# Loading the last of 32 output-weight blocks in two parts, ahead of the blocks before it

## The chip, the cores and the metric

The kernel runs on one core of one Trainium2 chip. The metric is the device time of one execution in microseconds (us); of several executions the median is taken.

## What is computed

One decoding step of an attention layer over a window of the key and value cache, times a gate from a small gated network. All data are float32. Batch B is 2, one query position, width D = 512, 32 query heads of 128, 8 key heads; the window is the last W = 4096 positions of 32768.

```python
def _A_ref(x, k_cache, v_cache, wq, wo):            # Hq 32, Dh 128
    q = (x @ wq).reshape(B, 1, Hq, Dh).transpose(0, 2, 1, 3)
    k = jnp.repeat(k_cache[:, :, Sk - W:, :], rep, axis=1)
    v = jnp.repeat(v_cache[:, :, Sk - W:, :], rep, axis=1)
    p = softmax(einsum("bhqd,bhkd->bhqk", q, k) * Dh ** -0.5)
    o = einsum("bhqk,bhkd->bhqd", p, v)
    return o.transpose(0, 2, 1, 3).reshape(B, 1, Hq * Dh) @ wo      # wo: 4096 x 512
s = _A_ref(layernorm(x), ...)
g = silu(_B_ref(layernorm(x), w_in, w_sp, b_sp, w_out))             # gated MLP, 512 -> 1792 -> 512
return x + s * g
```

The change concerns the last product, the attention output of 4096 numbers per batch entry by wo.

## The kernel before, in words

Everything is read once from memory and streamed through on-chip buffers. Large loads are issued by SyncE (SP) alone, in this order: wq in two halves, w_in, w_out, then for eight "units" (a unit is one batch entry and two key heads) a 4 MB load of keys and one of values, the values of a unit one step behind the keys, and at last wo. All of them go into a ring of four 32 KB-per-partition buffers (`slot`, L81), so that a load can be issued only when the buffer four loads earlier is free. wo's first buffer is the one that unit 5's values used, its second the one of unit 7's keys, its third the one of unit 6's values.

For each unit VectorE transposes the keys in 32x32 squares (`turn`), TensorE makes partial scores (`shares`, `add_shares`), VectorE and ScalarE make the softmax (`share_max`, `probs`), and TensorE weighs the values (`values`), after which ScalarE scales the result (`scale_out`) and TensorE adds it up by heads (`collect`). `gather` (L396) puts the output of one batch entry into `oT`: partition p, column n of its 32 columns holds row 32p + n of the 4096 rows of wo that it meets. It does so with four small TensorE products and one VectorE copy (L404 to L407). A "block" n of wo is therefore the 128 rows 32p + n, one for each partition, 256 KB; block n's product is `oT[:, n, :]` (128 x 32) by a tile of 128 x 512.

The loads of wo are written at L422 to L434: pieces of 8 and 8 blocks in the first buffer, 8 in the second, and 4, 2, 1 and 1 in the third. After the sixteenth block a 4 KB load of x stands in the queue (`x4`, L434).

The tail of the kernel (L480 to L501) uses two forms of the product:

- For blocks 0 to 27 (`EARLY = 28`) a block's product of 512 columns is added in one of four groups of 32 output rows of the tile `part`, group n % 4. ScalarE then copies `part` to `parts`, and `spread_quarters` (L276) adds the four groups with eight short products into `so`, 128 columns to a group.
- For blocks 28 to 31 four products of 128 columns each go straight to `so`. Blocks 28 and 29 stand before `spread_quarters`, blocks 30 and 31 behind it (`LATE = 30`).

VectorE multiplies `so` by the gate and adds x (`res`, L499 and L500), and SP stores 4 KB.

The order on each engine is the order of the program: `pe`, `dve`, `act` and `sp` are wrappers (`InOrder`, L27) that pass each call on and keep it in program order. For that reason the profile gives nearly all instructions the same line, L37, and groups are told apart by the names of their tiles. Each float32 product shows in the trace as two MATMUL records with a LDWEIGHTS record each: 28 blocks are 56 records of `part`.

Of the kernel before, what the change touches and what calls it, by code (L numbers as in the profile page):

```python
# [9 lines left out]
F32 = mybir.dt.float32  # L10
AF = mybir.ActivationFunctionType
# [3 lines left out]
P = 128  # L15
HQ, DH = 32, 128
G = 4
# [4 lines left out]
def ap(t, offset, dims):  # L22

    return bass.AP(tensor=t.tensor, offset=t.offset + offset, ap=[list(t.ap[0])] + [list(d) for d in dims])
# [18 lines left out]
def kernel(  # L43
# [13 lines left out]
    nc = tc.nc  # L57
    pe, dve, act, sp = (InOrder(tc, e) for e in (nc.tensor, nc.vector, nc.scalar, nc.sync))
    B, _, D = x.shape
# [17 lines left out]
    cst = ctx.enter_context(tc.tile_pool(name="cst", bufs=1))  # L77
# [3 lines left out]
    def slot(name):  # L81
        return ring.tile([P, SLOT], F32, tag="slot", name=name)

    def const(name, *shape):
        return cst.tile([P, *shape], F32, tag=name, name=name)

    def bank(name, tag):
        return ps.tile([P, 512], F32, tag=tag, name=name, bufs=BANKS[tag])
# [6 lines left out]
    for a in range(2):  # L95
        t = slot(f"wq{a}")
# [13 lines left out]
    def by_group(t):  # L110

        return bass.AP(tensor=t.tensor, offset=t.offset, ap=[[DC, G], [D, B], [1, DC]])
# [11 lines left out]
    ident = const("ident", P)  # L124
# [13 lines left out]
    place = const("place", 3 + P)  # L138
    nc.gpsimd.memset(place, 0.0)
    heads = const("heads", DH)  # L140
    oT = const("oT", 32, 32)
    nc.gpsimd.memset(oT, 0.0)

# [58 lines left out]
    for k in range(KT):  # L202
        for r in range(2):
            for g in range(G):
# [3 lines left out]
                    start=(k == 0), stop=(k == KT - 1),  # L208
# [19 lines left out]
    for k in range(KT):  # L228
        for g in range(G):
            pe.matmul(  # L230
                pz[32 * g : 32 * g + 32, :], xnT[:, k, :], ap(win[:, k, :], g * FQ, [[FH, 2], [1, FQ]]),
                start=(k == 0), stop=(k == KT - 1),
# [43 lines left out]
    def spread_quarters(dst, shares, start=True, stop=True):  # L276
        for g in range(G):
            pe.matmul(
                dst[32 * g : 32 * g + 32, :], rowm, shares[:, g * DC : (g + 1) * DC], start=start, stop=stop,
            )  # L280

    yp = bank("y", "sh")
    for j in range(FT):
        g = j % G
# [10 lines left out]
    dve.tensor_mul(gate, gate, y)  # L295


    def q_of(u, dq):
        return ap(qbd, (u.n * 4 + dq) * 32, [[1, 32]])

# [11 lines left out]
    def shares(u, m):  # L312

        u.sh = bank(f"sh{u.n}_{m}", "sh")
        for dq in range(4):
            pe.matmul(
                u.sh[32 * dq : 32 * dq + 32, :], q_of(u, dq), u.kt[m][:, :, 32 * dq : 32 * dq + 32],
                start=True, stop=True,
            )
        u.shs[m] = sb.tile([P, 512], F32, tag="shs", name=f"shs{u.n}_{m}")  # L320
        act.activation(u.shs[m], u.sh, AF.Copy)
# [99 lines left out]

    wo_v = wo.rearrange("(p j) d -> p j d", j=32)  # L422
    blocks = []
    pieces = ((8, 8), (8,), (4, 2, 1, 1))
    j = 0
    for i, piece in enumerate(pieces):
        t = slot(f"wo{i}").rearrange("p (j d) -> p j d", d=D)
        at = 0
        for n in piece:
            sp.dma_start(t[:, at : at + n, :], wo_v[:, j : j + n, :])  # L430
            blocks += [(t, at + a) for a in range(n)]
            at, j = at + n, j + n
            if j == 16:
                sp.dma_start(x4[0:P:16, :], by_group(x))  # L434

    prev = old = None
    last = units[-1]
# [39 lines left out]
    gather(last)  # L477


    EARLY, LATE = 28, 30  # L480
    part = bank("part", "sh")
    for n in range(EARLY):
        t, a = blocks[n]
        g = n % G
        pe.matmul(part[32 * g : 32 * g + 32, :], oT[:, n, :], t[:, a, :], start=(n < G), stop=(n >= EARLY - G))
    parts = sb.tile([P, D], F32, tag="shs", name="parts")
    act.activation(parts, part, AF.Copy)
    so = bank("so", "mo")[:, :DC]
    for n in range(EARLY, 32):
        if n == LATE:  # L490
            spread_quarters(so, parts, start=False, stop=False)
        t, a = blocks[n]
        for g in range(G):
            pe.matmul(
                so[32 * g : 32 * g + 32, :], oT[:, n, :], t[:, a, g * DC : (g + 1) * DC],
                start=(n == EARLY), stop=(n == 31),
            )
    res = const("res", DC)
    dve.tensor_mul(res, so, gate)  # L499
# [30 lines left out]
```

## Time and profile before

| What | Value |
|---|---|
| median of 3 runs | 217.53 us (217.28 to 217.55) |
| the profiled execution's own time | 217.5 us |
| its span, first to last instruction | 215.7 us |
| mean granted TensorE clock | 0.856 of full |
| read from memory | 89.40 MB |
| busy share of the span: TensorE, VectorE, ScalarE | 72%, 50%, 20% |

A row of the timeline has the start in us from the span's start, the duration from the first to the last end of the merged instructions, the engine (PE is TensorE, PEld its weight loads, DVE VectorE, ACT ScalarE, SPq the queue of SyncE), the operation, what it writes and reads, and in brackets how long the engine was idle before and what ended that. A row of the windows gives for each stretch of time the busy time of each engine, the granted TensorE clock, the share of time that the core's 16 DMA engines were busy, and GB/s.

### The profile page before, as it was taken

The page shows a single profiled execution, that of the slowest core. Times are in us where ns is not written, and L with a number is a line of the kernel's source. Part 1 is how long each engine was busy: PE and PEld are TensorE (multiplying, and loading weights), DVE is VectorE, ACT ScalarE, POOL GpSimd, SP SyncE. Part 2 cuts the span into 40 slices and gives each one's busy share as a digit, 9 for nine tenths or more (in the row PEclk, how much of TensorE's full clock was granted, in tenths as well). Part 3 has the DMA queues.
Part 4 walks back from the last instruction along what each step waited for, and adds up shares of the span by engine and source line. Part 5 has one row for each costly group of instructions (what it writes and reads, how often), then busy time and mean ns, then how long its engine had stood idle before and what let it go on. Part 6 is the DMA issues. An engine that isn't in the chain of part 4 may idle for free.

```text
span 215.7 us, 2229 instructions
## 1 busy us (share of the span) xinstructions
PE 155.7 (72%) x866; PEld 43.6 (20%) x866; DVE 108.5 (50%) x176; ACT 44.1 (20%) x109; POOL 2.6 (1%) x14
## 2 busy tenths in 40 slices
PE   0164856151796997899699599459959948998883
PEld 0110212110121222222122222222212212231311
DVE  3400072425976944963946851685577089240101
ACT  5000001401123115114303404120431421242001
POOL 4000000000000000000000000000000000000000
PEclk9999788755589699799889879958988995999699
DMA  7998999999999999999999999999999999999990
GB/s 292 389 486 389 425 433 454 451 416 431 444 395 474 395 459 413 450 425 431 437 400 456 413 444 428 431 437 431 431 407 453 419 444 431 431 401 416 425 377 35
DMA packets 3929, 89.54 MB, mean 415 GB/s; under 512 B 446, under 2 KB 462, under 8 KB 848
## 3 DMA queue, kind: packets, MB, share of 16 engines
q1 hardware_dynamic: 3912, 89.40, 96.8%
q8 instruction: 7, 0.11, 0.2%
q14 instruction: 2, 0.02, 0.0%
q10 hardware_dynamic: 8, 0.00, 0.0%
HBM read 89.40 MB, written 0.00 MB: 414 GB/s over the span
## 4 chain that ended last, share of the span: by engine, by line
DMA 44%; PE 31%; DVE 19%; issue 3%; ACT 1%; SPq 0%; DVEq 0%
DMA k<-in_A_k_cache_dram 22%; DMA win<-in_B_w_in_dram 14%; DVE kt L37 13%; PE s L37 9%; PE sh L37 9%; DMA wo<-in_A_wo_dram 8%; PE acc L37 6%; PE z L37 2%; PE y L37 2%; PE mo L37 1%; DVE gate L37 1%; PE col L37 1%; PE so L37 1%; DVE u L37 1%; DVE m L37 1%
## 5 line engine op out<-in xcount | busy, mean ns | idle before, releaser
L37 DVE STREAM_TRANSPOSE kt<-k 128x2048 f32<-128x2048 f32 x32 | 72.4, 2293 | 24.9 <-DMA k<-in_A_k_cache_dram 24.9
L37 PE MATMUL sh<-kt,qbd 128*32 128x512 f32 x256 | 41.5, 682 | 14.0 <-DVE kt L37 14.0
L37 PE MATMUL s<-shs,add_dq 128*128 128x512 f32 x64 | 41.0, 748 | 0.0
L37 ACT ACTIVATE shs<-sh 128x512 f32<-128x512 f32 x32 | 19.1, 597 | 100.9 <-PE sh L37 100.9
L37 PE MATMUL acc<-v,pT 128*32 128x512 f32 x256 | 32.0, 641 | 0.2 <-DVE pT L37 0.2
L37 PE MATMUL q_ps<-wq,xnT 128*32 128x512 f32 x64 | 11.0, 850 | 9.9 <-DMA wq<-in_A_wq_dram 9.9
L37 PEld LDWEIGHTS s<-shs,add_dq 128*128 128x128 f32 x64 | 11.2, 219 | 28.3 <-issue 23.9
L37 PEld LDWEIGHTS sh<-kt,qbd 128*32 128x32 f32 x256 | 6.9, 115 | 33.9 <-issue 19.6
L37 PEld LDWEIGHTS acc<-v,pT 128*32 128x32 f32 x256 | 7.7, 118 | 25.8 <-issue 23.0
L37 DVE TENSOR_REDUCE m<-s 128x2 f32<-128x512 f32 x8 | 5.4, 680 | 14.0 <-PE s L37 14.0
L37 PE MATMUL mo<-l,same_r 128*128 128x2 f32 x16 | 3.5, 287 | 10.7 <-ACT p L37 10.7
L37 DVE STREAM_TRANSPOSE qT<-q_ps 128x512 f32<-128x512 f32 x2 | 1.4, 717 | 18.1 <-PE q_ps L37 18.1
L37 ACT ACTIVATE o<-acc,wd 128x128 f32<-128x128 f32 x32 | 9.1, 373 | 3.4 <-PE acc L37 3.4
L37 ACT ACTIVATE p<-s,nb 128x256 f32<-128x256 f32 x16 | 7.6, 490 | 7.1 <-DVE nb L37 6.9
L37 PE MATMUL part<-wo,oT 128*32 128x512 f32 x56 | 8.2, 722 | 1.1 <-DMA wo<-in_A_wo_dram 0.8
L37 PE MATMUL col<-o,sel 128*32 128x512 f32 x16 | 8.3, 601 | 0.4 <-ACT o L37 0.4
L37 ACT ACTIVATE zs<-z 128x448 f32<-128x448 f32 x1 | 0.5, 544 | 30.9 <-PE z L37 30.9
L37 PE MATMUL y<-wout,hT 128*32 128x512 f32 x14 | 3.6, 1059 | 3.8 <-issue 3.8
L37 PEld LDWEIGHTS q_ps<-wq,xnT 128*32 128x32 f32 x64 | 2.6, 144 | 17.1 <-issue 12.2
L37 DVE STREAM_TRANSPOSE pT<-p 128x512 f32<-128x512 f32 x8 | 5.4, 675 | 1.2 <-ACT p L37 1.2
L37 DVE TENSOR_TENSOR res<-so,gate 128x128 f32<-128x128 f32 x1 | 0.3, 292 | 11.1 <-PE so L37 11.1
L37 ACT ACT_TABLE_LOAD x4 | 5.1, 1283 | 1.9 <-issue 1.9
(106 smaller groups left out, 66.8 us busy)
## 6 DMA issues: line engine op xcount, KB each, us to landing
k<-in_A_k_cache_dram SPq DMA_DIRECT2D x8, 4096.0 KB, 21.3
v<-in_A_v_cache_dram SPq DMA_DIRECT2D x8, 4096.0 KB, 26.7
wq<-in_A_wq_dram SPq DMA_DIRECT2D x2, 4096.0 KB, 21.3
wo<-in_A_wo_dram SPq DMA_DIRECT2D x3, 2048.0 KB
win<-in_B_w_in_dram SPq DMA_DIRECT2D x1, 3584.0 KB, 29.3
wout<-in_B_w_out_dram SPq DMA_DIRECT2D x1, 1792.0 KB, 33.1
wo<-in_A_wo_dram SPq DMA_DIRECT2D x1, 1024.0 KB
wo<-in_A_wo_dram SPq DMA_DIRECT2D x1, 512.0 KB, 17.4
```

The source lines that it names most:

```text
L37: return self.tc.keep_in_program_order(call(*args, **kwargs))
```

## The change

Block 31 no longer comes last and no longer as one load of 256 KB.

- `woe` is a tile of 128 x 512 that GpSimd clears at the start; block 31's rows of the even partitions (64 rows, 128 KB) are loaded into its even partitions.
- `woo` is a tile of 32 partitions with two rows of 512 each; the rows of the odd partitions (64 rows, 128 KB) are loaded there, two to a partition. The load's source is written as 8 x 8 rows, the outer step 64 rows and the inner 512 rows.
- Both loads are issued behind the second buffer's 8 blocks and ahead of the third buffer's pieces, which are now 4, 2 and 1 blocks.
- The first sixteen blocks are one load of 4 MB in place of two of 2 MB.
- `odd` is a matrix of zeros and ones that ScalarE copies from the identity once, behind the gate. After the last `gather`, two products with it pick the odd partitions of `oT[:, 31, :]` in the order of `woo`, and ScalarE copies each result to `oTo`.
- Block 31 moves from the short form to the long one: three products (even rows with `woe`, and two of 32 rows with `woo`) are added to `part` behind block 27, in groups 0, 1 and 2. Behind `spread_quarters` only block 30 is left.

```diff
+    woe = const("woe", D)
+    nc.gpsimd.memset(woe, 0.0)
+    woo = cst.tile([G * 8, 2, D], F32, tag="woo", name="woo")
+    oTo = const("oTo", 2, 32)
+    odd = const("odd", 2, 8, G)
     oT = const("oT", 32, 32)
     nc.gpsimd.memset(oT, 0.0)
...
+    act.activation(odd, ap(ident, 1, [[16, 2], [2, 8], [32, G]]), AF.Copy)
...
-    pieces = ((8, 8), (8,), (4, 2, 1, 1))
+    pieces = ((16,), (8,), (4, 2, 1))
...
             if j == 16:
                 sp.dma_start(x4[0:P:16, :], by_group(x))
+            if j == 24:
+                sp.dma_start(woe[0:P:2], wo_v[0:P:2, 31, :])
+                sp.dma_start(
+                    woo.rearrange("p s d -> p (s d)"),
+                    bass.AP(tensor=wo.tensor, offset=wo.offset + 63 * D, ap=[[64 * D, 8], [512 * D, 8], [1, D]]),
+                )
...
+    for a in range(2):
+        t = bank(f"oTo{a}", "acc")[: G * 8, :32]
+        pe.matmul(t, odd[:, a].rearrange("p o i -> p (o i)"), oT[:, 31, :], start=True, stop=True)
+        act.activation(oTo[: G * 8, a, :], t, AF.Copy)
     EARLY, LATE = 28, 30
+    early = [(oT[:, n, :], blocks[n][0][:, blocks[n][1], :]) for n in range(EARLY)]
+    early += [(oT[:, 31, :], woe)] + [(oTo[: G * 8, a, :], woo[:, a, :]) for a in range(2)]
     part = bank("part", "sh")
-    for n in range(EARLY):
-        t, a = blocks[n]
+    for n, (o, w) in enumerate(early):
         g = n % G
-        pe.matmul(part[32 * g : 32 * g + 32, :], oT[:, n, :], t[:, a, :], start=(n < G), stop=(n >= EARLY - G))
+        pe.matmul(part[32 * g : 32 * g + 32, :], o, w, start=(n < G), stop=(n >= len(early) - G))
     parts = sb.tile([P, D], F32, tag="shs", name="parts")
     act.activation(parts, part, AF.Copy)
     so = bank("so", "mo")[:, :DC]
-    for n in range(EARLY, 32):
+    for n in range(EARLY, 31):
...
-                start=(n == EARLY), stop=(n == 31),
+                start=(n == EARLY), stop=(n == 30),
```

## The prediction

> **What bounds the kernel now.** I read the page first, its slices of time and its chain, then the timeline of the tail, then the tail in windows of half a microsecond, and last SP's own timeline.
>
> ```profile
> span 215.7 us, 2229 instructions
> DMA  7998999999999999999999999999999999999990
> HBM read 89.40 MB, written 0.00 MB: 414 GB/s over the span
> ```
>
> The DMA engines are busy in all slices but the last. The kernel is a stream of 89.40 MB at 414 GB/s with a tail behind it, so what an edit in the last loads is worth is decided behind the point at which that stream thins out. The tail in the timeline (the first columns are the start and the duration):
>
> ```profile
> 200.07 1.07 PE L37 MATMUL oT<-heads,place 32*128 32x32 f32 x8 [0.78 <-DVE heads L37]
> 201.18 0.21 DVE L37 COPY oT<-oT 128x32 f32<-128x32 f32 x1 [1.17 <-PE oT L37]
> 201.49 5.24 PE L37 MATMUL part<-wo,oT 128*32 128x512 f32 x32 [0.35 <-issue]
> ...
> 205.26 0.13 PEld L37 LDWEIGHTS part<-wo,oT 128*32 128x32 f32 x4 [0.30 <-issue]
> 205.69 0.13 PEld L37 LDWEIGHTS part<-wo,oT 128*32 128x32 f32 x4 [0.30 <-issue]
> ...
> 206.96 1.92 PE L37 MATMUL part<-wo,oT 128*32 128x512 f32 x16 [0.23 <-DMA wo<-in_A_wo_dram]
> ...
> 209.45 1.07 PE L37 MATMUL part<-wo,oT 128*32 128x512 f32 x8 [0.57 <-DMA wo<-in_A_wo_dram]
> 210.65 0.60 ACT L37 ACTIVATE parts<-part 128x512 f32<-128x512 f32 x1 [12.45 <-PE part L37]
> ...
> 210.70 0.64 PE L37 MATMUL so<-wo,oT 128*32 128x128 f32 x16 [0.18 <-DMA wo<-in_A_wo_dram]
> 211.29 0.16 PEld L37 LDWEIGHTS so<-parts,rowm 128*32 128x32 f32 x8 [0.22 <-ACT parts L37]
> 211.30 0.43 PE L37 MATMUL so<-parts,rowm 128*32 128x128 f32 x8
> ...
> 211.54 0.86 PE L37 MATMUL so<-wo,oT 128*32 128x128 f32 x16
> 211.97 0.16 PEld L37 LDWEIGHTS so<-wo,oT 128*32 128x32 f32 x8 [0.30 <-DMA wo<-in_A_wo_dram]
> 212.46 0.29 DVE L37 TENSOR_TENSOR res<-so,gate 128x128 f32<-128x128 f32 x1 [11.07 <-PE so L37]
> ```
>
> TensorE waits for each piece of wo: at 206.96 for the second buffer, at 209.45 for blocks 24 to 27, at 210.70 for 28 and 29, at 211.97 for block 31. Two chains run side by side here. The one by transfer ends with block 31: landed, 211.97, its products, `res` at 212.46. The other starts with blocks 24 to 27: 209.45, their products until 210.52, ScalarE's copy 210.65 to 211.25, the spreading from 211.30, block 30 from 211.54. The second chain reaches block 31 only 0.30 us before the first; that 0.30 of idle weight-load time is all that the transfer's end holds up by itself. A change that helps the transfer and lengthens the other chain has at most this much to gain.
>
> The stream does not end on all engines at once:
>
> ```profile
> 209.00:209.50 0.50, 0.05 (x4) 0.05 (x8) 0.00 (x0) 0.00 (x0) 0.00 (x0) 1.00 1.07 414
> 209.50:210.00 0.50, 0.50 (x8) 0.11 (x8) 0.00 (x0) 0.00 (x0) 0.00 (x0) 1.00 0.64 246
> 210.00:210.50 0.50, 0.50 (x8) 0.00 (x0) 0.00 (x0) 0.00 (x0) 0.00 (x0) 1.00 0.49 188
> 210.50:211.00 0.50, 0.32 (x15) 0.30 (x16) 0.00 (x0) 0.35 (x1) 0.00 (x0) 1.00 0.42 160
> 211.00:211.50 0.50, 0.50 (x23) 0.28 (x16) 0.00 (x0) 0.24 (x1) 0.00 (x0) 1.00 0.31 119
> 211.50:212.00 0.50, 0.47 (x20) 0.20 (x13) 0.00 (x0) 0.00 (x0) 0.00 (x0) 1.00 0.00 0
> ```
>
> The last two figures are the DMA share and GB/s. The share is full until 209.5, about a half from 210, and nothing after 211.5: some eight of sixteen engines have ended their work by 210 and the others carry on for about 1.5 us. As every engine has an equal part of each of these loads, one half lags the other by that much, and each wait of TensorE above is a wait for the lagging half.
>
> **The change part by part.** Loads first. From the waits, 512 KB (blocks 28 and 29) end 210.70 - 209.45 = 1.25 us behind the piece before, so 256 KB on sixteen engines take 0.63 us and 128 KB take 0.31. `woe` (128 KB on sixteen engines) puts 0.31 us ahead of blocks 24 to 27 on every engine. `woo` (128 KB) is twice as dense if eight engines carry it: 0.63 us on those eight, nothing on the others. Blocks 24 to 27 therefore come 0.31 us later if `woo` falls to the leading half (that half is then 0.94 us later, which its lead of about 1.5 covers) and 0.94 later if it falls on even one lagging engine. I take 0.31; no row of the profile names the engine of a transfer, so 0.94 stays as the upper end. [...]
>
> The new issues on SP cost nothing:
>
> ```profile
> 167.80 0.81 SPq L37 DMA_DIRECT2D wo<-in_A_wo_dram  x2
> 168.66 0.66 SPq L37 DMA_DIRECT2D x<-in_A_x_dram  x1
> 184.86 9.81 SPq L37 DMA_DIRECT2D wo<-in_A_wo_dram  x5
> ```
>
> Two issues take 0.81 us, x's 0.66. The row of five covers the second buffer's load at 184.86 and, some 9 us on, the third buffer's pieces, which wait for their buffer. `woe` and `woo` have tiles of their own, wait for no buffer and are issued in that gap; what is queued behind them on SP are those same pieces, which cannot go earlier. Their cover is that wait; without it they would cost about 1 us of issue, still far ahead of the 20 us in which the queue works off what it holds. One load of sixteen blocks in place of two carries the same bytes: zero for the stream. But blocks 0 to 7 now wait for block 15 too: 8 blocks of the second buffer are 2.1 MB, at 414 GB/s 5.1 us, so the first buffer is complete at about 206.96 - 5.1 = 201.9, where TensorE began at 201.49.
>
> Ahead of block 0 TensorE has two new products of 32 columns. The nearest row is `oT`: eight records of 32 columns in 1.07 us, so four records 0.54, between 0.3 and 1.1. They lie in the wait just named. Block 0 starts at 201.49 + 0.54 = 202.03 in place of 201.49. The sixteen blocks took until 206.73, so they end by 207.3, the next eight without a wait by 207.3 + 1.92 = 209.2. Blocks 24 to 27 come at 209.45 + 0.31 = 209.76: the 0.54 is hidden by 0.56 us of waiting. Even 1.1 would show only as hundredths of a microsecond. ScalarE's copies to `oTo` (two of the size below the `parts` copy of 0.60) have 8 us until their product is due; the copy to `odd` and GpSimd's clearing of `woe` come within the first quarter of the span, where neither engine is on the chain.
>
> Then the products that count. In the long form eight blocks took 1.92 us and four 1.07, so four more cost 0.85. The weight loads show how: in fours, 205.26 and 205.69, 0.43 apart, each four being one record for each of the four groups, so two such rounds for four blocks. The three new products lie in groups 0, 1 and 2: three quarters of the width, but each group still takes its two rounds. That makes 0.85; if the price went by block it would be 0.64. I take 0.85, because the rounds are in the rows. What is taken away is block 31 behind the spreading: its 0.30 of waiting and its eight short records, 0.24 (block 30 starts 0.24 after the spreading's first record, which is the price of eight).
>
> The sum, along the second chain: blocks 24 to 27 at 209.76; seven blocks, counted as two full pairs of rounds, 1.92, until 211.68; ScalarE's copy starts 0.13 later (as 210.65 follows 210.52) and ends at 212.41; the spreading at 212.46; block 30 at 212.70. Blocks 28 and 29 fit in between, as their 0.64 falls while ScalarE copies. The last block's products need 0.49 until `res` (211.97 to 212.46), so `res` comes at 213.19 in place of 212.46: 0.73 later, or some hundredths less, as block 30 follows without a restart. I say 0.7. The last transfer would land at 211.97 - 0.31 = 211.66, more than 1 us before it is used. Behind `res` nothing changes. The profiled execution took 217.5 us with a span of 215.7, and the median of the runs is 217.53: 217.5 + 0.7 = 218.2. With the lower prices (0.64 for the products) it is 218.0.
>
> **The rivals.**
>
> *`woo` meets lagging engines.* Blocks 24 to 27 land 0.94 later, 0.63 more than in my sum, all of it on the chain: 218.8. [...] For it: no row ties the lagging half to a number. [...]
>
> *Not slower: the new products go into the gap.* TensorE is idle from about 209.2 (208.7 if the front costs nothing) to 209.76. Were the three products done there, blocks 24 to 27 would end at 210.83, the copy at 211.56, the spreading start at 211.61, block 30 at 211.85, `res` at 212.34, 0.12 earlier than before: 217.4. It decides if the gap is over 0.85 and the order on TensorE lets them ahead. Their data would be there, as it stands ahead in the queue. Against it: they are written behind block 27, and the rows above show `so` and `part` in the order of the program throughout.
>
> *Faster: the lag is smaller.* If the lagging half were a microsecond less behind in the changed kernel, blocks 24 to 27 would land by 208.8. TensorE itself comes to them at 209.2 at the earliest by my front, 208.7 with a free one, so `res` would come 1.06 earlier than in my sum at the most: 217.1 to 217.6. Nothing in the change touches what makes the engines lag.
>
> *The clock.* Over the stretches of one clock period:
>
> ```profile
> 197.95:201.36 3.41, 2.12 (x10) 1.10 (x10) 0.86 (x2) 0.24 (x1) 0.00 (x0) 1.00 0.95 400
> 201.36:204.78 3.42, 3.29 (x16) 0.90 (x20) 0.03 (x1) 0.00 (x0) 0.00 (x0) 0.50 1.02 434
> 204.78:208.19 3.41, 3.18 (x32) 0.82 (x28) 0.00 (x0) 0.00 (x0) 0.00 (x0) 1.00 0.97 404
> 208.19:211.60 3.41, 2.66 (x44) 0.84 (x40) 0.00 (x0) 0.60 (x1) 0.00 (x0) 1.00 0.66 257
> ```
>
> After a stretch with 2.12 us of TensorE work the clock fell to 0.50; after one with 2.66 it stayed full. In the changed kernel the stretch to 211.60 holds a similar amount (0.9 until 209.1, 1.84 from 209.76), so I expect no fall. If it fell there, the four rounds of 0.43 would take twice that: 1.7 us more, 219.9. [...]
>
> **How the numbers follow.** A measurement of this kernel can tell about 0.2%, 0.44 us, from no change. My sum 58%, its own range 217.9 to 218.4; about 10 of these 58 lie within 0.44 us, if the cheaper prices hold together. `woo` on lagging engines or slow: 24%, all slower. The gap: 10%, 8 within and 2 faster. A smaller lag: 4%, faster. The clock: 4%, slower. So slower 0.48 + 0.24 + 0.04 = 0.76, within 0.18, faster 0.06. The range reaches from 217.7, a little under the cheap end of my sum, to 218.9, past `woo` on lagging engines; it leaves out the gap, the smaller lag and the clock, 18%.
>
> **What would show it.** Right: `part` has 62 records; its last row begins at about 209.8 and holds seven blocks, 14 records, in about 1.9 us with no wait inside; the copy to `parts` starts near 211.8; the last `so` records wait for `parts`, not for a transfer; the DMA share in the last stretch falls more evenly, to nothing by about 211.2. `woo` on lagging engines would show as a wait for blocks 24 to 27 until about 210.4 with a thin DMA share behind it. The gap would show as records of `woe` before 209.7. I am wrong if `res` waits for a transfer at its end, or if the copy to `parts` is over by 211.5.

## The result and the profile after

The changed kernel takes 219.47 us (median of 6 runs, 219.21 to 219.53) against 217.54 for the kernel before on the same chip: a ratio of 1.0089, 95% interval 1.0076 to 1.0102. It is slower by 1.93 us, on the side that was forecast, and above the range of 217.7 to 218.9. The profiled execution took 219.43 us.

The page of the profiled execution, its span and its chain:

```profile
span 217.6 us, 2237 instructions
DMA k<-in_A_k_cache_dram 23%; DMA win<-in_B_w_in_dram 14%; DVE kt L37 13%; PE s L37 9%; PE sh L37 8%; DMA wo<-in_A_wo_dram 8%; PE acc L37 6%; PE y L37 2%; PE z L37 1%; PE part L37 1%; PE mo L37 1%; DVE gate L37 1%; PE col L37 1%; DVE u L37 1%; DVE m L37 1%
```

`PE part` now stands in the chain that ended last; before, the end belonged to `PE so` behind a transfer. The tail in the timeline of the changed kernel, to be laid beside the rows of the prediction:

```profile
201.17 0.40 PE L37 MATMUL oTo<-oT,odd 128*32 128x32 f32 x4 [0.40 <-DVE oT L37]
...
202.01 7.81 PE L37 MATMUL part<-wo,oT 128*32 128x512 f32 x48 [0.44 <-DMA wo<-in_A_wo_dram]
...
210.03 1.06 PE L37 MATMUL part<-wo,oT 128*32 128x512 f32 x8 [0.21 <-DMA wo<-in_A_wo_dram]
...
210.91 1.02 PE L37 MATMUL part<-woe,oT 128*32 128x512 f32 x2
...
211.86 0.14 PEld L37 LDWEIGHTS part<-woo,oTo 32*32 32x32 f32 x4 [0.84 <-issue]
211.86 1.05 PE L37 MATMUL part<-woo,oTo 32*32 32x512 f32 x4
212.84 0.38 PEld L37 LDWEIGHTS so<-wo,oT 128*32 128x32 f32 x16 [0.84 <-issue]
...
212.98 0.60 ACT L37 ACTIVATE parts<-part 128x512 f32<-128x512 f32 x1 [11.19 <-PE part L37]
213.63 0.16 PEld L37 LDWEIGHTS so<-parts,rowm 128*32 128x32 f32 x8 [0.42 <-ACT parts L37]
...
213.88 0.40 PE L37 MATMUL so<-wo,oT 128*32 128x128 f32 x8
214.34 0.29 DVE L37 TENSOR_TENSOR res<-so,gate 128x128 f32<-128x128 f32 x1 [13.32 <-PE so L37]
```

`res` starts at 214.34 in place of 212.46, 1.88 later; that is the difference of the spans, 217.6 - 215.7 = 1.9. Two rows differ from the sum of the prediction. Blocks 24 to 27 are waited for until 210.03, not 209.76. And the products of block 31 do not share their two rounds: `woe` starts its two at 210.91, the two of `woo` start theirs together only at 211.86, and what follows them starts at 212.84, each step about 0.95 us. At the last two steps the weight loads name no wait for data, only `issue`, with 0.84 us of idle each time. The mark `32*32` on the `woo` rows is the form of the product: 32 rows by 32 columns, where all others in the tail have `128*32`.

The transfers, in the last windows of the same kernel (share of the DMA engines and GB/s last):

```profile
209.50:210.00 0.50, 0.32 (x4) 0.00 (x0) 0.00 (x0) 0.00 (x0) 0.00 (x0) 1.00 0.83 332
210.00:210.50 0.50, 0.47 (x7) 0.17 (x9) 0.00 (x0) 0.00 (x0) 0.00 (x0) 1.00 0.55 217
210.50:211.00 0.50, 0.50 (x9) 0.18 (x2) 0.00 (x0) 0.00 (x0) 0.00 (x0) 1.00 0.46 180
211.00:211.50 0.50, 0.50 (x6) 0.02 (x1) 0.00 (x0) 0.00 (x0) 0.00 (x0) 1.00 0.09 33
211.50:212.00 0.50, 0.50 (x4) 0.14 (x4) 0.00 (x0) 0.00 (x0) 0.00 (x0) 1.00 0.11 33
```

Before, the share was 0.64 from 209.5 and 0.31 from 211.0; now it is 0.83 and 0.09, so the work of the engines is spread a little more evenly. The end did not move by an amount that can be told. The trace also keeps the times at which the parts of a load report their landing, sixteen for a load of 128 partitions, as many as the core has DMA engines; each is read here as one engine's part. The last part of the last load landed at 211.85, and in the kernel before at 211.93. Two kernels below that keep all loads of the third buffer as before had 211.79 and 211.83. And nothing waits for the last piece any more.

The same records show how the engines stood before the change. Of blocks 24 to 27 eight parts landed between 207.49 and 207.72, two at 208.23 and 208.70, and six between 209.16 and 209.41. So the prediction's leading half is there, and behind it are two engines in between and six that lag by 1.4 to 1.9 us.

### The profile page after: what moved, and what is told of

Its sections match the earlier page's. It is cut to its first block, busy times and chain, and to the rows that moved or that the text cites. A ratio compares the mean times of both kernels' runs of the same rounds, so it can differ in the third digit from the quotient of the medians.

```text
span 217.6 us, 2237 instructions
## 1 busy us (share of the span) xinstructions
PE 156.7 (72%) x868; PEld 43.5 (20%) x868; DVE 108.6 (50%) x176; ACT 44.5 (20%) x112; POOL 3.1 (1%) x15
## 4 chain that ended last, share of the span: by engine, by line
DMA 44%; PE 31%; DVE 19%; issue 3%; ACT 1%; SPq 0%; DVEq 0%
DMA k<-in_A_k_cache_dram 23%; DMA win<-in_B_w_in_dram 14%; DVE kt L37 13%; PE s L37 9%; PE sh L37 8%; DMA wo<-in_A_wo_dram 8%; PE acc L37 6%; PE y L37 2%; PE z L37 1%; PE part L37 1%; PE mo L37 1%; DVE gate L37 1%; PE col L37 1%; DVE u L37 1%; DVE m L37 1%
## 5 line engine op out<-in xcount | busy, mean ns | idle before, releaser
L37 PE MATMUL sh<-kt,qbd 128*32 128x512 f32 x256 | 40.4, 670 | 14.4 <-DVE kt L37 14.4
L37 PE MATMUL s<-shs,add_dq 128*128 128x512 f32 x64 | 39.7, 727 | 0.0
L37 PE MATMUL acc<-v,pT 128*32 128x512 f32 x256 | 34.3, 681 | 0.2 <-DVE pT L37 0.2
L37 PE MATMUL q_ps<-wq,xnT 128*32 128x512 f32 x64 | 10.4, 809 | 10.2 <-DMA wq<-in_A_wq_dram 10.2
L37 PEld LDWEIGHTS s<-shs,add_dq 128*128 128x128 f32 x64 | 10.5, 205 | 27.7 <-issue 23.3
L37 PE MATMUL part<-wo,oT 128*32 128x512 f32 x56 | 8.9, 788 | 0.7 <-DMA wo<-in_A_wo_dram 0.7
```

What stands on the lines that cost most here:

```text
L37: return self.tc.keep_in_program_order(call(*args, **kwargs))
```

## The experiments

The theory after the result has two parts. A: a product of 32 rows does not run beside the products of 128 rows before it, and the other way round. C: one of the eight engines that the prediction gave to `woo`'s load lags, and it is the last for blocks 24 to 27. The rival to A (B): three products are slow because they fill few groups or stand one behind another, whatever their rows.

**All products with 128 rows.** The tiles of the odd rows get zeros below the 32 partitions used:

```diff
-    woo = cst.tile([G * 8, 2, D], F32, tag="woo", name="woo")
+    woo = const("woo", 2, D)
+    nc.gpsimd.memset(woo, 0.0)
     oTo = const("oTo", 2, 32)
+    nc.gpsimd.memset(oTo, 0.0)
...
-    early += [(oT[:, 31, :], woe)] + [(oTo[: G * 8, a, :], woo[:, a, :]) for a in range(2)]
+    early += [(oT[:, 31, :], woe)] + [(oTo[:, a, :], woo[:, a, :]) for a in range(2)]
```

> woo and oTo are widened to 128 partitions with zeros below the 32 used, so that block 31's three products all have 128 rows; the loads are those of the changed kernel. Theory A (a product of 32 rows doesn't run beside one of 128): the 14 records of part behind the wait for blocks 24 to 27 take 1.92 us from first to last end, not 2.93, the copy to parts starts about 1.0 us earlier, and the kernel takes 218.5. Rival B (the three products are slow because they lie one behind another or fill only three groups, whatever their rows): the records still take 2.6 to 2.9 us and the kernel stays at 219.4. The wait for blocks 24 to 27 stays at about 210.0 in both.

Measured: 218.48 us, 1.0039 of the kernel before (1.0024 to 1.0053). Its timeline:

```profile
209.74 0.21 PEld L37 LDWEIGHTS part<-wo,oT 128*32 128x32 f32 x8 [0.65 <-DMA wo<-in_A_wo_dram]
...
210.69 0.59 PE L37 MATMUL part<-woe,oT 128*32 128x512 f32 x1
...
210.69 0.59 PE L37 MATMUL part<-woo,oTo 128*32 128x512 f32 x2
...
211.12 0.59 PE L37 MATMUL part<-woe,oT 128*32 128x512 f32 x1
211.12 0.60 PE L37 MATMUL part<-woo,oTo 128*32 128x512 f32 x2
...
211.83 0.60 ACT L37 ACTIVATE parts<-part 128x512 f32<-128x512 f32 x1 [10.33 <-PE part L37]
...
213.19 0.29 DVE L37 TENSOR_TENSOR res<-so,gate 128x128 f32<-128x128 f32 x1 [12.46 <-PE so L37]
```

`woe` and both of `woo` now start together, in two rounds at 210.69 and 211.12, 0.43 apart. From the wait for blocks 24 to 27 to the copy of `parts` are 211.83 - 209.74 = 2.09 us; in the changed kernel 212.98 - 210.03 = 2.95. B is refuted: same products, same groups, same order, only the rows differ. The wait ended at 209.74, where 210.0 was expected; this execution took 218.15 us, the fastest of six, and 0.33 less than their median.

**The row forms alternated.** The other direction, twice the suspected cost:

```diff
-    early += [(oT[:, 31, :], woe)] + [(oTo[: G * 8, a, :], woo[:, a, :]) for a in range(2)]
+    odds = [(oTo[: G * 8, a, :], woo[:, a, :]) for a in range(2)]
+    early += [odds[0], (oT[:, 31, :], woe), odds[1]]
```

> The changed kernel with its three products of block 31 in the order 32 rows, 128 rows, 32 rows, in place of 128, 32, 32: three changes of the row form behind block 27 and not one. Theory A (a product waits until those of the other row form have drained): all three products now stand alone, each about 0.95 us; the copy to parts starts about 4.0 us behind the wait for blocks 24 to 27 (2.95 in the changed kernel), and the kernel takes 220.5. Rival B (slow because few groups are filled, or because of the load or the copy that feeds the 32-row products): the order makes no difference, 219.5.

Measured: 220.43 us, ratio 1.0134 (1.0118 to 1.0149). TensorE's timeline:

```profile
210.09 1.07 PE L37 MATMUL part<-wo,oT 128*32 128x512 f32 x8 [1.05 <-DMA wo<-in_A_wo_dram]
211.09 1.04 PE L37 MATMUL part<-woo,oTo 32*32 32x512 f32 x2
212.06 1.04 PE L37 MATMUL part<-woe,oT 128*32 128x512 f32 x2
213.04 1.04 PE L37 MATMUL part<-woo,oTo 32*32 32x512 f32 x2
214.01 0.64 PE L37 MATMUL so<-wo,oT 128*32 128x128 f32 x16
```

The same three products, each alone now with its two rounds, start 0.97 to 0.98 us apart, and the copy to `parts`, at 214.12 in this kernel, is 4.03 behind the wait. A holds in both directions.

**The products left out.** Block 31's share is missing from the output; loads and picking products stay:

```diff
-    early += [(oT[:, 31, :], woe)] + [(oTo[: G * 8, a, :], woo[:, a, :]) for a in range(2)]
```

> The three products of block 31 are left out (so block 31's share is missing from the output); its two loads, the two picking products ahead of block 0 and their copies stay. Theory A: without them the tail from the wait for blocks 24 to 27 is what it was before less block 31: copy to parts 1.2 us behind the wait, res about 2.5 us behind it; 219.47 - 1.85 = 217.6. Rival C (the transfers or the late half clock make the loss): the wait for blocks 24 to 27 or TensorE's arrival there holds the end, and the kernel stays above 218.5.

Measured: 217.76 us against 217.47 before, ratio 1.0007 (0.9996 to 1.0018; the quotient of the two medians is 1.0013). The wait and the copy in its timeline:

```profile
210.00 0.16 PEld L37 LDWEIGHTS part<-wo,oT 128*32 128x32 f32 x8 [0.85 <-DMA wo<-in_A_wo_dram]
211.20 0.60 ACT L37 ACTIVATE parts<-part 128x512 f32<-128x512 f32 x1 [9.38 <-PE part L37]
```

The three products are thus worth 219.47 - 217.76 = 1.71 us of the 1.93. The loads cost their delay here too, and it is paid back almost in full because no block 31 stands behind the spreading.

**Block 31 in one part.** One load on all engines in the same place, one product, no picking products:

```diff
-                sp.dma_start(woe[0:P:2], wo_v[0:P:2, 31, :])
...
+                sp.dma_start(woe, wo_v[:, 31, :])
...
-    early += [(oT[:, 31, :], woe)] + [(oTo[: G * 8, a, :], woo[:, a, :]) for a in range(2)]
+    early += [(oT[:, 31, :], woe)]
```

> Block 31 as one load of 256 KB over all engines at the place of the two, and one product of 128 rows behind block 27; no picking products. Theory A: no change of the row form; the wait for blocks 24 to 27 ends 0.63 us later than before (210.1), five blocks take 1.06 + 0.85 = 1.92 us there, and the kernel takes 218.4 to 218.6. Rival B: a product alone in its group is as slow as in the changed kernel (1.0 us), about the same 218.5; so the time doesn't tell, but the length of that one product does: 0.85 more than four blocks by A. If the eight-engine load helps blocks 24 to 27, their wait ends later here than in the changed kernel by about 0.3 us.

Measured: 218.48 us, 1.0042 (1.0027 to 1.0058). The wait and the copy in its timeline:

```profile
210.18 0.16 PEld L37 LDWEIGHTS part<-wo,oT 128*32 128x32 f32 x8 [0.76 <-DMA wo<-in_A_wo_dram]
...
212.18 0.60 ACT L37 ACTIVATE parts<-part 128x512 f32<-128x512 f32 x1 [14.09 <-PE part L37]
```

From the wait to the copy are 2.00 us for five blocks, where seven took 2.09 with 128 rows: the price goes by rounds and hardly by the number of groups filled. Moving block 31 ahead in plain form already costs 1.0 us. The wait ends at 210.18, 0.15 behind that of the changed kernel, not 0.3; this execution took 218.66 us, 0.18 above the median.

**The first sixteen blocks in one load, alone.** The kernel before with this edit:

```diff
-    pieces = ((8, 8), (8,), (4, 2, 1, 1))
+    pieces = ((16,), (8,), (4, 2, 1, 1))
```

> The kernel before with one change alone: the first sixteen blocks in one load. All theories: no difference beyond 0.1%, 217.5. Block 0 then starts at about 202.0 instead of 201.5, and this is hidden by the wait for the second buffer. If the single load by itself costs or gains over 0.2%, the sums of all theories are wrong by that.

Measured: 217.54 us, ratio 0.9998 (0.9988 to 1.0008). The first sixteen blocks and the next eight, and its last wait for a transfer:

```profile
202.04 6.74 PE L37 MATMUL part<-wo,oT 128*32 128x512 f32 x48 [0.93 <-DMA wo<-in_A_wo_dram]
211.83 0.16 PEld L37 LDWEIGHTS so<-wo,oT 128*32 128x32 f32 x8 [0.27 <-DMA wo<-in_A_wo_dram]
```

The first product of `part` started at 202.04 and the delay went into the wait for the second buffer, as expected.

**The odd rows loaded twice.** The second load goes into a tile that nothing reads:

```diff
+                sp.dma_start(
+                    wo2.rearrange("p s d -> p (s d)"),
+                    bass.AP(tensor=wo.tensor, offset=wo.offset + 63 * D, ap=[[64 * D, 8], [512 * D, 8], [1, D]]),
+                )
```

> The changed kernel with the load of the odd rows issued twice, the second time into a tile that nothing reads (same engines, 128 KB more). If at least one of its eight engines lags (theory C), blocks 24 to 27 are waited for about 0.6 us longer, until 210.6, and the kernel takes 220.1. If all eight lead by over 1 us (the sum of the prediction), their wait stays at 210.0 and the kernel at 219.5.

Measured: 220.19 us, 1.0123 (1.0107 to 1.0138). The wait in its timeline:

```profile
210.69 1.06 PE L37 MATMUL part<-wo,oT 128*32 128x512 f32 x8 [1.46 <-DMA wo<-in_A_wo_dram]
```

The wait grew by 0.66 us, about the 0.63 that the prediction reckoned for 128 KB on eight engines. With the lead of about 1.5 that it gave to all eight, the wait would not have moved. The landings of the parts confirm this and show how many engines it is. In the changed kernel `woo` has eight landings between 206.01 and 207.49 (and one entry at 187.06, right behind its issue), and of blocks 24 to 27 the last part landed at 209.99, 0.25 behind the one before it (209.74). With the odd rows loaded twice the last part landed at 210.65, 0.81 behind the one before it (209.84). So, with each part read as one engine's, the odd rows hold up one engine beyond the rest, and the others end earlier. That the second load ran on the engines of the first is not in the trace; a last part that landed 0.66 later, where 0.63 was reckoned, fits it for the engine that ends last. The issue of blocks 24 to 27 came at 193.48 here and at 192.33 in the changed kernel, but both are 14 us or more ahead of the first landing (207.88 and 207.92), so it does not explain the wait.

**Without the odd rows.** Their load, the picking products and their two products are left out (block 31's odd rows are missing from the output):

```diff
-                sp.dma_start(
-                    woo.rearrange("p s d -> p (s d)"),
...
-    early += [(oT[:, 31, :], woe)] + [(oTo[: G * 8, a, :], woo[:, a, :]) for a in range(2)]
+    early += [(oT[:, 31, :], woe)]
```

> The changed kernel without the odd rows: their load, the picking products and the two products of 32 rows are left out (block 31's odd rows are missing from the output); the even rows' load and product stay. Theory C (one of the eight engines lags and is the last for blocks 24 to 27): their wait ends at 209.7, 0.3 us earlier than in the changed kernel, and the even rows' product takes 0.85 us behind them as in the one-part kernel: res near 213.1, 218.1. Rival: the eight-engine load costs this wait nothing, which then ends at 210.0 here too.

Measured: 218.22 us, 1.0037 (1.0024 to 1.0050). The wait in its timeline:

```profile
209.66 0.16 PEld L37 LDWEIGHTS part<-wo,oT 128*32 128x32 f32 x8 [1.82 <-DMA wo<-in_A_wo_dram]
```

With `woe` alone the wait ends 0.21 behind that of the kernel before, with `woo` 0.58 behind it in the changed kernel. C fits both runs: without `woo` the last two parts of blocks 24 to 27 landed together, both at 209.62. How far the one engine lags differs by some tenths from one execution to another: with both loads, the waits ended at 210.03, 210.00, 210.09 and, in the kernel with 128 rows, 209.74, where the last part came only 0.01 behind the one before it.

**A version without the two faults.** The odd rows' products have 128 rows and stand behind block 23; `woe` is loaded and multiplied last; blocks 24 to 30 take the short form:

```diff
-    EARLY, LATE = 28, 30
+    EARLY, LATE = 24, 30
...
-    early += [(oT[:, 31, :], woe)] + [(oTo[: G * 8, a, :], woo[:, a, :]) for a in range(2)]
+    early += [(oTo[:, a, :], woo[:, a, :]) for a in range(2)]
...
+            if j == 31:
+                sp.dma_start(woe[0:P:2], wo_v[0:P:2, 31, :])
...
```

> All three findings put together: the odd rows' products have 128 rows (zeros below the 32) and stand behind block 23, ahead of the wait for blocks 24 to 27; block 31's even rows are loaded last and multiplied last in the short form; blocks 24 to 30 take the short form too, so that the copy to parts starts before the last pieces land. By theories A and C the products fall out of the chain and only the balance of the transfers is left: res follows the last landing by 0.5 us, and the last landing comes 0.05 to 0.3 us earlier than in the kernel before: 217.2 to 217.5. If a shorter chain behind blocks 24 to 27 isn't what counts, it stays above 218.

Measured: 217.59 us, 1.0006 (0.9997 to 1.0015), above the 217.2 to 217.5 that were expected. In its timeline TensorE came to the new products only at 209.66:

```profile
201.89 7.94 PE L37 MATMUL part<-wo,oT 128*32 128x512 f32 x48 [0.73 <-DMA wo<-in_A_wo_dram]
209.66 0.59 PE L37 MATMUL part<-woo,oTo 128*32 128x512 f32 x2
...
212.73 0.29 DVE L37 TENSOR_TENSOR res<-so,gate 128x128 f32<-128x128 f32 x1 [12.11 <-PE so L37]
```

A window of the same execution shows why (the granted clock is the third figure from the end):

```profile
203.50:207.00 3.50, 3.50 (x20) 0.79 (x16) 0.00 (x0) 0.00 (x0) 0.00 (x0) 0.50 0.96 400
```

TensorE worked through all of this window at half clock. The kernel with the single load alone started the same 48 products no earlier (at 202.04, this one at 201.89), but had full speed again from 204.7 (a granted clock of 0.82 over 203.50 to 207.00, where this one has 0.50) and was through them at 208.78, where this one took until 209.83. So the clock made TensorE late here, and not the single load.

**The same with the first load in two again**, so that TensorE starts earlier:

```diff
-    pieces = ((16,), (8,), (4, 2, 1))
+    pieces = ((8, 8), (8,), (4, 2, 1))
```

> The version with the odd rows' products ahead of the wait for blocks 24 to 27, with one edit: the first sixteen blocks in two loads again, so that TensorE starts on block 0 at about 201.2 and not at 201.9. If TensorE's late arrival (209.66 there) is what took the gain, it arrives by 209.2, the short products end with the transfers, res comes at 212.2 to 212.4 and the kernel takes 217.1 to 217.4. If the last landing on the one lagging engine sets the end, it stays at 217.5.

Measured: 217.66 us, 1.0003 (0.9994 to 1.0011). Its timeline:

```profile
208.76 1.03 PE L37 MATMUL part<-woo,oTo 128*32 128x512 f32 x4
...
211.84 0.16 PEld L37 LDWEIGHTS so<-woe,oT 128*32 128x32 f32 x8 [0.19 <-DMA woe<-in_A_wo_dram]
...
212.34 0.29 DVE L37 TENSOR_TENSOR res<-so,gate 128x128 f32<-128x128 f32 x1 [11.65 <-PE so L37]
```

TensorE is early now and the end belongs to the last transfer again, at 211.84. The kernel before had 211.97, but with its loads of the third buffer unchanged the wait ended at 211.83 and 211.87 in the kernel with the single load alone and in the next one. So no earlier landing is shown, and the expected 217.1 to 217.4 did not come. TensorE's earlier arrival is not the edit's alone either, as the clock was back at full speed from about 203.9: its rounds start 0.85 us apart up to 203.51 and 0.43 from 204.13 on.

**The kernel before with a shorter chain of products**, loads unchanged:

```diff
-    EARLY, LATE = 28, 30
+    EARLY, LATE = 24, 30
```

> The kernel before with blocks 24 to 27 in the short form too, loads unchanged. It shortens the chain by products alone and leaves the one by transfer. The prediction read that the chain by products reached block 31 0.30 us ahead of its landing, so there is nothing to gain: 217.5, res still about 0.5 us behind the last wait. If it is faster by over 0.1%, that reading was wrong.

Measured: 217.45 us, 0.9996 (0.9987 to 1.0005). Its last wait for a transfer:

```profile
211.87 0.16 PEld L37 LDWEIGHTS so<-wo,oT 128*32 128x32 f32 x8 [0.42 <-DMA wo<-in_A_wo_dram]
```

`res` came 0.49 later: the chain by transfer sets this end, as the prediction read it. No version here beats the kernel before.

## Why the prediction was wrong

The direction and the chain were right: the change lengthened the chain that starts with blocks 24 to 27, and the transfers gained nothing. The direction did not hang on the step that failed, as the two kernels with nothing but 128 rows in `part` are slower by 1.0 us too. The size was not: 0.7 forecast, 1.93 measured. In the profiled executions `res` came 1.15 us behind the sum's 213.19, and the rows divide this: 0.27 in the wait for blocks 24 to 27 (210.03 for 209.76), 0.90 from there to the copy (2.95 for 211.81 - 209.76 = 2.05), and -0.02 from the copy to `res` (1.36 for 1.38).

The step that failed is "seven blocks, counted as two full pairs of rounds, 1.92". Its premise was that the three new products run side by side as `part`'s other blocks do. The row it went by holds only products of 128 rows; the `woo` products have 32. With 128 rows for all, the step holds: that kernel needs 2.09 us from the wait to the copy, where the sum has 2.05. That its copy at 211.83 and its `res` at 213.19 are the very figures of the sum is luck in part, as the wait of this execution ended early; its median of 218.48 is above the forecast 218.2. With the forms alternated each product stands alone. That the change of form is the cause is shown by these two runs: from the wait to the copy are 2.09 us with one form and 4.03 with the forms alternated, where the changed kernel has 2.95. The alternated kernel gives the price: from a product of 512 columns, alone with its two rounds of 0.43, to the next of another form are 0.97 us. So by this difference the change of form itself costs about 0.1 (0.97 - 0.86), and the rounds that can't be shared cost most: the two of `woo` came behind those of `woe`, 0.86 of the 0.90. The sum should have had a rival for this, as the `32*128` rows of `oT` in the profile before are another form too.

The second mis-sized term is the delay of blocks 24 to 27: 0.31 forecast, 0.58 measured. That eight engines carry `woo` and the others nothing was the author's assumption, which no row of the profile before shows; what the runs show in its place is eight landings of its load in the changed kernel. The sum put all eight in the leading half; the rival put a fully lagging engine there, at 0.94. The runs show something between: one of the eight ends last, but it stood ahead of the last engine before `woo` came, as `woo` moved the wait by 0.37 behind the kernel without it (210.03 for 209.66). Loading the odd rows twice moved the wait by 0.66, and the landings show one part alone behind the others in both kernels, by 0.25 and 0.81. The prediction read the share of one half as one half of the engines ahead of the other; the landings in the kernel before show eight parts ahead, two in between and six behind. Which engine it is, and why it lags, no run here shows. The last landing was mis-sized too, 211.85 where the sum had 211.66, but nothing waited for it.

Of the signs that the prediction named for being right, the 62 records of `part` came, and the last `so` records wait for `parts` and not for a transfer. The seven blocks in about 1.9 us and the copy near 211.8 did not come: they took 2.88 us (210.03 to 212.91), and the copy started at 212.98.

The other steps held. The issues on SP cost nothing (0.50 us for `woe` at 185.28 and 0.81 for `woo` at 185.84, while the pieces behind them were issued only from 192.33); the single load of sixteen blocks is 0.9998; block 0 started at 202.01, forecast 202.03. The cover of the front was thinner than it looked: TensorE's clock was at half until 207, and it was done with the blocks ahead at 209.82, with 0.21 us to spare, where the sum had 209.2 and 0.56:

```profile
205.00:205.50 0.50, 0.50 (x8) 0.08 (x4) 0.00 (x0) 0.00 (x0) 0.00 (x0) 0.50 1.14 463
206.50:207.00 0.50, 0.50 (x5) 0.00 (x0) 0.00 (x0) 0.00 (x0) 0.00 (x0) 0.50 0.99 401
207.00:207.50 0.50, 0.50 (x8) 0.12 (x4) 0.00 (x0) 0.00 (x0) 0.00 (x0) 1.00 1.03 426
```

These windows of the changed kernel show 0.50 in the column of the clock until 207, where the kernel before had full speed from 204.78. The rival of the clock looked for this in the tail; it came at the front, where the wait for blocks 24 to 27 hid it, but only because that wait was longer than forecast: the sum's landing at 209.76 would have come before TensorE. How long the clock stays at half differs between the executions: 3.42 us in the kernel before (201.36 to 204.78), 6.82 here (200.18 to 207.00), and in the kernel without the odd rows not at all from block 0 on, whose rounds start 0.43 us apart from 202.00.

Of the rivals, the gap did not occur: the records stand in the order of the program. Put there by hand, the products did fit (208.76 to 209.79 in the version with two first loads), and no gain remained.

## What to carry to other kernels

Before giving a product fewer rows to suit a load, look at the form marks of its neighbours in the trace: here a product of another form waited for theirs and let none of them run beside it (0.97 us for each alone), and rows filled up with zeros were cheaper than fewer rows, 218.48 us for 219.47. And before moving work ahead of a transfer, follow the chain that starts at the piece it is put before: here a gain of at most 0.30 us at the end was bought with a delay of 0.58 us and four rounds of products, two of them for the other form, on the chain beside it.

## What the runs showed of the hardware

A product of 32 rows in the tail cost 0.97 us alone, the same as one of 128 rows alone (1.04 from start to end in both, the alternated kernel), and three of 128 rows side by side took no longer (210.69 to 211.72, all rows at 128). The sixteen parts of one load did not land together: in the kernel before, eight parts of blocks 24 to 27 landed by 207.72 and the last six between 209.16 and 209.41. The two loads ahead did not bring the last landing forward: 211.85 in the changed kernel, 211.79 to 211.93 in three executions without the two loads.
